# Attention and channel mix on one core: the five engines' order lists searched anew

## The chip, the core and the metric

The kernel runs on one core of a Trainium2 chip. The metric is the device time of one execution in microseconds, the median of several runs; lower is better. A core has five instruction streams: TensorE (PE; its weight loads are shown as PEld), VectorE (DVE), ScalarE (ACT), GpSimd (POOL) and SyncE (SP). Each works off its own list in order and meets the others through semaphores. In this kernel POOL issues the loads, SP the stores and the DMA transposes.

## The reference

Batch 8, 8 heads, 576 tokens, head size 64. A sliding-window attention with a linear position bias feeds a channel mix:

```python
scores = scale * np.matmul(q, k.transpose(0, 1, 3, 2))          # per head, 576 x 576
mask = (rel >= 0) & (rel < 128)                                  # rel = query - key
attn = softmax(np.where(mask, scores + bias, -1e9))              # bias = -slope * |rel|
x = np.matmul(attn, v)                                           # heads side by side: 576 x 512
xk = mu_k * x + (1 - mu_k) * x_prev                              # x_prev: the token before
xr = mu_r * x + (1 - mu_r) * x_prev
k = np.maximum(xk @ w_k, 0)                                      # 512 -> 1024
out = sigmoid(xr @ w_r) * ((k * k) @ w_v)                        # 1024 -> 512
```

## The kernel before, in words

Attention runs over 32 pairs of heads: pair `it` is heads 2g and 2g+1 of batch b = it // 4. The channel mix runs over units of two batches (P = 0 to 3, 1152 tokens each), cut into column chunks (c0) and row tiles (c) of 128 tokens. The program first registers 1139 small operations with their engine, dependencies and the buffer ring that they take a slot of. A planner then issues them. For each engine a text list, `ORDER`, gives the order in which its operations must be issued; each operation may start only after the one before it in the list. So the lists are the program's order on each engine, and the waits between engines follow from dependencies and rings. The planner's costs only settle how the five lists interleave when the program is written.

The names in the lists, with the kernel line that shows them in the profile:

- POOL: `lql.b.w.i` loads q (i = 0) or k (i = 1) of half of a batch's heads by token (L130), `lqp`, part of batch 0 (L119), `lqn.b.i.j` a block of 128 tokens for batches 4 to 7 (L88), `lts.b.i` the last 64 tokens (L124), `lvs.b.j` the blocks of V (L110, the last one L114), `lwk`, `lwr`, `lwv` the weights. `clear0`, `ms` and `clear` set ones and zeros in buffers (L441 to L447, L873, L875).
- SP: `lq`, `lmu` first loads; `tr.b.i` the DMA transpose of q or k of batch b in 4 to 7 (L93), `trt.b.i` of its tail (L98); `st.P.c` the store of a tile (L371).
- PE: `tq`, `tk`, `tail` transposes (L158, L171), `score.it.e` the scores of half of the keys (L219; pairs 0 to 3 add the bias by a matmul, L198), `av` (L250), `ot` the transpose of the result (L270), `m1.P.c0.fo` the product with w_k (L313; `m1a` its first three matmuls), `m3.P.c` with w_r (L336), `m2a` and `m2` the two halves of the product with w_v (L351; the last two tiles in column halves, L358), `fill` filler matmuls on zeros (L182), `tmu` a small transpose.
- ACT: `mask0` (L415), `pq` copies of q and k out of PSUM (L138), `exp` (L227), `xt` (L275), `rl` the relu (L319), `rs` the gate (L342), a few squares `kk`.
- DVE: `c`, `ct` casts by token (L149), `pk` (L135), `mcopy`, `dcopy`, `sid`, `id8`, `cmu` (constants), `mask` (L232), `norm` (L261, L262), `xk` (L295 and L302), `xr` (L302), `kk` the square (L328), `oo`, `oob` the product with the gate (L366).

Rings and buffers that couple the lists: `sa` (2 slots) holds scores and AV products in PSUM, `mm` (3 slots) the products of m1, m2 and m3, `ot` (4 slots) the tiles that wait for their store, three buffers hold V by batch, two hold q and k by batch (`ql`), and one (`qt`) holds the transposed q and k of a batch in 4 to 7. So `lqn` of batch 4 waits until `ct` of batch 2 has read the buffer, `lqn` of batch 6 until `tr` of batch 4 has, and `tr` of batch b until all scores of batch b-1 that used `qt` are done.

Of the kernel before, what the change touches and what calls it, by code (L numbers as in the profile page):

```python
# [16 lines left out]
def kernel(  # L17
# [704 lines left out]
    for i, m in enumerate(FILL):  # L722
# [4 lines left out]
            tq.0 tk.0 fill.0 tq.2 tail.0 score.0.0 score.2.0 tq.3 tmu score.2.1 score.0.1 av.2.0  # L727
            av.0.0 tq.1 score.3.0 score.3.1 av.0.1 ot.0.0 score.1.0 av.3.0 ot.0.1 av.2.1 tail.1
            ot.2.0 score.1.1 av.1.0 ot.3.0 av.3.1 ot.2.1 fill.1 av.1.1 ot.1.0 fill.2 ot.1.1
            m1a.0.0.0 ot.3.1 m1.0.0.0 m1.0.0.3 m1.0.0.2 tq.4 m1a.0.0.1 m1.0.0.4 m1.0.0.1 m1.0.0.5  # L730
            score.4.0 score.4.1 m1.0.256.0 tq.5 m1.0.256.3 m1.0.256.6 score.5.0 score.5.1 m1.0.0.6
            m1.0.256.5 m1.0.256.4 tq.6 m1.0.256.7 av.4 score.6.0 m1.0.256.1 ot.4 av.5 score.6.1
            tq.7 m3.0.2 m3.0.1 m1.0.256.2 ot.5 score.7.1 score.7.0 tail.2 m1.0.0.7 m3.0.0 tq.8
            av.6 m3.0.3 av.7 tq.9 m2a.0.0 m2a.0.1 ot.6 score.8.1 score.8.0 m2a.0.3 ot.7 m2.0.0
            m2.0.1 score.9.1 score.9.0 m2.0.3 m1.0.512.0 tq.10 m1.0.512.4 m1.0.512.1 m1.0.512.2
            av.8 m1.0.512.5 m2a.0.2 score.10.1 score.10.0 m1.0.512.7 ot.8 m2.0.2 av.9 tq.11
            m1.0.512.6 m1.0.512.3 m3.0.4 score.11.1 score.11.0 m3.0.8 ot.9 m3.0.6 m3.0.5 tq.12
            m1.0.768.0 av.10 m1.0.768.1 tq.13 m1.0.768.2 m1.0.768.7 score.12.0 score.13.0 m2a.0.4
            tail.3 ot.10 av.11 m2.0.4 tq.14 score.12.1 m2a.0.5 score.14.1 tq.15 m2.0.5 score.13.1
            score.14.0 m1.0.768.3 ot.11 m1.0.768.5 av.12 m1.0.768.4 m1.0.768.6 score.15.0  # L740
            score.15.1 m3.0.7 ot.12 av.13 m1.1.0.0 av.14 score.17.0 m1.1.0.7 score.18.0 score.16.1
            m2a.0.6 score.18.1 m2.0.6 score.17.1 m2a.0.7 av.15 score.16.0 m1.1.0.5 ot.13
            score.19.1 score.19.0 m2a.0.8 m2.0.7 ot.14 m2.0.8 m3.1.1 ot.15 m1.1.0.1 m1.1.0.6
            m3.1.0 m3.1.2 m1.1.0.4 m3.1.3 av.17 m1.1.512.0 av.16 m1.1.0.2 m1.1.512.7 m1.1.0.3
            m1.1.512.4 m1.1.512.3 ot.16 av.18 av.19 m2a.1.2 m2a.1.3 ot.17 m2a.1.0 m2.1.2 m2.1.0
            m2.1.3 ot.18 m2a.1.1 score.21.1 score.20.0 ot.19 m2.1.1 score.22.1 m1.1.512.5
            m1.1.512.2 score.20.1 m3.1.4 m1.1.896.0 score.23.1 score.22.0 m3.1.6 m3.1.8 m1.1.512.6
            m1.1.512.1 score.21.0 score.23.0 m3.1.5 m1.1.896.2 m3.1.7 av.20 m2a.1.6 m1.1.896.6
            m2.1.6 ot.20 av.21 m1.1.896.4 m1.1.896.7 m2a.1.5 av.22 m2a.1.4 m2.1.5 ot.21 m2.1.4
            m1.1.896.3 m1.2.0.0 m1.1.896.1 m1.2.0.4 m1.2.0.1 m1.2.0.3 m1.1.896.5 m1.2.0.7 ot.22  # L750
            av.23 m3.2.0 m1.2.0.5 m1.2.0.2 m3.2.1 ot.23 m2a.1.8 m1.2.0.6 score.27.1 score.24.1
            m2.1.8 m3.2.2 score.25.0 score.26.0 m2a.1.7 m2a.2.0 score.26.1 score.25.1 m2.1.7
            m2a.2.1 score.24.0 score.27.0 m2.2.0 m2.2.1 m1.2.512.0 m3.2.3 m1.2.512.7 m1.2.512.6
            m1.2.512.5 m2a.2.3 av.24 m2a.2.2 m2.2.3 m3.2.6 m2.2.2 av.25 ot.24 m1.2.896.0 m3.2.4
            m1.2.512.2 m1.2.512.3 m1.2.512.4 av.26 m1.2.896.6 m1.2.896.7 m1.2.512.1 ot.25
            m1.2.896.1 m3.2.8 m1.2.896.3 m3.2.5 av.27 m1.2.896.5 ot.26 m3.2.7 m1.2.896.4 ot.27
            m2a.2.5 score.29.0 score.28.0 m2.2.5 m2a.2.4 score.31.1 score.28.1 m2.2.4 m2a.2.6
            score.30.0 score.29.1 m2.2.6 m1.2.896.2 m1.3.0.0 score.30.1 score.31.0 m1.3.0.1
            m1.3.0.5 av.28 m1.3.0.6 m3.3.2 m1.3.0.2 m1.3.0.4 ot.28 av.29 m3.3.3 m1.3.0.7 m1.3.0.3
            ot.29 m2a.2.8 av.30 m2.2.8 m2a.2.7 ot.30 av.31 m2.2.7 m3.3.0 m3.3.1 m2a.3.2 ot.31  # L760
            m2a.3.3 m2.3.2 m2.3.3 m1.3.512.0 m2a.3.1 m2a.3.0 m2.3.1 m2.3.0 m1.3.512.2 m1.3.512.1
            m1.3.512.7 m3.3.4 m3.3.8 m1.3.512.5 m1.3.512.4 m1.3.512.6 m1.3.512.3 m1.3.896.0 m3.3.7
            m1.3.896.7 m3.3.5 m1.3.896.2 m2a.3.5 m2a.3.4 m2.3.5 m2.3.4 m1.3.896.1 m3.3.6
            m1.3.896.3 m1.3.896.6 m1.3.896.5 m2a.3.6 m1.3.896.4 m2.3.6 m2a.3.8 m2.3.8 m2a.3.7
            m2.3.7
        """,
        "ACT": """
            mask0.6 pq.0 mask0.4 mask0.2 mask0.0 pq.2 exp.0.0 exp.2.0 pq.3 exp.2.1 exp.0.1 pq.1
            exp.3.0 xt.0.0 exp.3.1 xt.0.1 exp.1.0 xt.2.0 xt.3.0 exp.1.1 xt.2.1 xt.1.0 xt.1.1
            xt.3.1 rl.0.0.0 rl.0.0.3 rl.0.0.2 pq.4 rl.0.0.4 rl.0.0.1 rl.0.0.5 exp.4.0 exp.4.1 pq.5  # L770
            rl.0.256.0 rl.0.256.3 rl.0.256.6 exp.5.0 rl.0.0.6 exp.5.1 pq.6 rl.0.256.5 rl.0.256.4
            exp.6.0 xt.4 rl.0.256.1 rl.0.256.7 exp.6.1 pq.7 rs.0.2 rs.0.1 rl.0.256.2 xt.5 exp.7.1
            exp.7.0 pq.8 rl.0.0.7 rs.0.3 rs.0.0 pq.9 xt.6 exp.8.1 xt.7 exp.8.0 exp.9.1 exp.9.0
            rl.0.512.0 rl.0.512.4 rl.0.512.1 kk.0.512.1 pq.10 rl.0.512.2 rl.0.512.5 exp.10.1 xt.8
            kk.0.512.5 exp.10.0 rl.0.512.7 pq.11 rl.0.512.3 rl.0.512.6 rs.0.4 exp.11.1 rs.0.8 xt.9
            rs.0.6 exp.11.0 pq.12 rs.0.5 rl.0.768.0 rl.0.768.1 pq.13 rl.0.768.2 kk.0.768.1
            exp.12.0 rl.0.768.7 xt.10 exp.13.0 pq.14 exp.12.1 exp.14.1 pq.15 exp.13.1 xt.11
            rl.0.768.3 exp.14.0 rl.0.768.5 rl.0.768.4 exp.15.0 kk.0.768.5 exp.15.1 rl.0.768.6
            rs.0.7 rl.1.0.0 exp.17.0 exp.18.0 exp.16.1 exp.18.1 exp.17.1 rl.1.0.7 xt.12 exp.16.0
            rl.1.0.5 kk.1.0.5 xt.13 xt.14 exp.19.1 xt.15 rs.1.1 rl.1.0.1 kk.1.0.1 rl.1.0.6 rs.1.0  # L780
            rs.1.2 exp.19.0 rs.1.3 rl.1.0.4 rl.1.512.0 rl.1.0.2 rl.1.512.7 rl.1.0.3 rl.1.512.4
            rl.1.512.3 xt.16 xt.17 xt.18 exp.21.1 exp.20.0 exp.22.1 rl.1.512.5 rl.1.512.2 exp.20.1
            kk.1.512.5 rl.1.896.0 rs.1.4 exp.23.1 rs.1.6 exp.22.0 rs.1.8 rl.1.512.6 rl.1.512.1
            exp.21.0 kk.1.512.1 rs.1.5 xt.19 rl.1.896.2 exp.23.0 rs.1.7 rl.1.896.6 rl.1.896.4
            rl.1.896.7 xt.20 rl.1.896.3 rl.2.0.0 rl.1.896.1 rl.2.0.4 kk.1.896.1 rl.2.0.1 xt.21
            kk.2.0.1 rl.1.896.5 rl.2.0.3 rl.2.0.7 kk.1.896.5 rs.2.0 rl.2.0.5 xt.22 rl.2.0.2
# [6 lines left out]
            exp.31.0 rl.3.0.2 rs.3.2 xt.28 rl.3.0.4 rs.3.3 rl.3.0.3 rl.3.0.7 xt.29 xt.30 rs.3.0
            rs.3.1 xt.31 rl.3.512.0 rl.3.512.2 rl.3.512.1 rl.3.512.7 rs.3.4 rs.3.8 rl.3.512.5
            rl.3.512.4 rl.3.512.6 rl.3.512.3 rl.3.896.0 rs.3.7 rl.3.896.7 rs.3.5 rl.3.896.2
            rl.3.896.1 rs.3.6 rl.3.896.3 rl.3.896.6 rl.3.896.5 rl.3.896.4
        """,
        "DVE": """
            id8 c.0.0 c.0.1 sid dcopy pk.0 ct.2 mcopy.2 pk.2 tcopy.0 ct.3 pk.3 ct.1 cmu mcopy.1
            norm.0.0 pk.1 mcopy.0 norm.2.0 norm.0.1 xk.0.0 norm.3.0 norm.2.1 tcopy.1 norm.1.0 ct.4  # L800
            xk.2.0 norm.3.1 norm.1.1 xk.1.0 xk.3.0 xk.2.1 xk.1.1 kk.0.0.0 xk.0.1 kk.0.0.2 kk.0.0.3
            xk.3.1 ct.5 kk.0.0.4 kk.0.0.1 xr.3 kk.0.0.5 xr.2 xr.1 ct.6 mask.4.0 kk.0.256.0
# [193 lines left out]
```

## Time and profile before

| what | value |
|---|---|
| median of 3 runs | 238.65 us (238.22 to 239.57) |
| the profiled execution, first to last instruction | 237.9 us |
| PE busy | 223.9 us, 94% |
| DVE busy | 193.2 us, 81% |
| ACT busy | 165.7 us, 70% |
| POOL busy | 93.2 us, 39% |
| chain that ended last | PE 76%, DVE 13%, DMA 3%, ACT 3% |
| DMA | 31.56 MB in 114810 packets |

No separate time is given for the profiled execution; its span is 0.75 us below the median of the runs. Busy is the share of the span in which an engine had an instruction in work. A row of the timeline gives the start in us, the length in us, the engine, the line, the operation, out<-in, the shape and the count; in brackets the idle time of the engine before it and what ended it. The granted clock of TensorE is 1.000 throughout.

### The profile page before, as it was taken

To read this page: it belongs to the slowest core of one execution; us is meant where nothing else is said; L and a number is where in the kernel's file an instruction comes from. 1 tells how busy PE (TensorE), PEld (TensorE's weight loads), DVE (VectorE), ACT (ScalarE), POOL (GpSimd) and SP (SyncE) were. 2 spreads that over 40 slices of the span, in tenths; PEclk is the share of its full clock that TensorE was granted. 3 is DMA by queue.
4 is the path that set the end of the run, shared out by engine and by line. 5 is a ranking of instruction groups with operands and counts; after the bars stand their busy time and mean duration, and the time that the engine had idled before them with its cause. 6 is when DMAs were issued, how large, how long until landed. Compare 5 with 4: busy or idle time off the path is not lost.

```text
span 237.9 us, 5426 instructions
## 1 busy us (share of the span) xinstructions
PE 223.9 (94%) x2130; PEld 132.9 (56%) x2163; DVE 193.2 (81%) x406; ACT 165.7 (70%) x281; POOL 93.2 (39%) x131
## 2 busy tenths in 40 slices
...
GB/s 131 166 137 184 178 160 200 188 159 210 202 139 149 134 164 135 125 123 212 193 171 184 123 123 181 193 77 148 99 90 3 118 19 0 91 0 132 0 91 178
DMA packets 114810, 31.56 MB, mean 133 GB/s; under 512 B 99160, under 2 KB 110432, under 8 KB 114784
## 3 DMA queue, kind: packets, MB, share of 16 engines
...
## 4 chain that ended last, share of the span: by engine, by line
PE 76%; DVE 13%; DMA 3%; ACT 3%; issue 2%; POOL 1%; POOLq 0%; DVEq 0%
PE pv L351 23%; PE ps L313 22%; PE pr L336 13%; PE sa L250 6%; PE sa L219 5%; PE tp L270 3%; DMA ql<-in_k_dram 3%; DVE at L232 2%; DVE xu L262 2%; DVE xk L302 2%; ACT at L227 2%; PE pv L358 1%; PE tp L158 1%; DVE ct L149 1%; DVE xr L302 1%
## 5 line engine op out<-in xcount | busy, mean ns | idle before, releaser
L313 PE MATMUL ps<-xk,wk_sb 128*128 128x256 bf16 (+2 forms) x410 | 71.9, 313 | 0.7 <-DVE xk L302 0.4
L319 ACT ACTIVATE rl<-ps 128x256 bf16<-128x256 f32 (+2 forms) x104 | 47.6, 476 | 31.1 <-PE ps L313 27.0
L227 ACT ACTIVATE at<-sa 128x1024 bf16<-128x1024 f32 x64 | 64.3, 1035 | 4.1 <-PE sa L219 3.9
L351 PE MATMUL pv<-wv_sb,kk 128*128 128x512 bf16 x257 | 63.9, 379 | 1.3 <-issue 0.6
L313 PEld LDWEIGHTS <-wk_sb 128*128 128x128 bf16 x416 | 38.7, 98 | 24.2 <-issue 2.0
L351 PEld LDWEIGHTS <-kk 128*128 128x128 bf16 x272 | 24.3, 98 | 24.3 <-issue 1.5
L232 DVE TENSOR_TENSOR at<-at,mask 128x1024 bf16<-128x1024 bf16 x56 | 37.5, 683 | 0.5 <-ACT at L227 0.2
L328 DVE TENSOR_TENSOR kk<-rl 128x256 bf16<-128x256 bf16 (+2 forms) x88 | 28.3, 335 | 10.7 <-ACT rl L319 10.1
L336 PE MATMUL pr<-wr_sb,xr 128*128 128x512 bf16 x135 | 35.6, 380 | 0.5
L366 DVE SCALAR_TENSOR_TENSOR ot<-rs,pv 128x512 f32<-128x512 bf16 (+1 forms) x38 | 24.5, 656 | 11.2 <-PE pv L351 4.9
L110 POOL DMA_DIRECT2D vs<-in_v_dram x32 | 28.6, 904 | 6.0 <-PE tp L270 2.4
L275 ACT COPY xt<-tp 128x576 bf16<-128x576 bf16 (+2 forms) x36 | 21.3, 590 | 13.4 <-PE tp L270 13.3
L302 DVE SCALAR_TENSOR_TENSOR xk<-dl,mu_sb,xt 128x576 bf16<-128x576 bf16 (+2 forms) x36 | 27.1, 752 | 1.3
L342 ACT ACTIVATE rs<-pr 128x512 bf16<-128x512 f32 x36 | 21.7, 611 | 8.8 <-PE pr L336 8.7
L302 DVE SCALAR_TENSOR_TENSOR xr<-dl,mu_sb,xt 128x576 bf16<-128x576 bf16 x32 | 25.5, 811 | 0.0
L250 PEld LDWEIGHTS <-at 128*128 128x128 bf16 x576 | 21.2, 98 | 6.4 <-issue 2.4
L262 DVE TENSOR_TENSOR xu<-sa,rc 128x640 bf16<-128x640 f32 x28 | 23.1, 824 | 1.0
L250 PE MATMUL sa<-vs,at 128*128 128x65 bf16 x448 | 18.9, 194 | 1.9 <-ACT rl L319 1.9
L336 PEld LDWEIGHTS <-xr 128*128 128x128 bf16 x144 | 13.4, 98 | 13.0 <-issue 0.6
L88 POOL DMA_DIRECT2D ql<-in_k_dram x16 | 14.2, 894 | 14.8 <-DMA qt<-ql 11.0
L138 ACT COPY qk<-tp 128x1024 bf16<-128x1024 bf16 (+1 forms) x16 | 14.7, 917 | 6.1 <-DVE qk L135 3.8
L295 DVE TENSOR_TENSOR dl<-xt 128x576 bf16<-128x576 bf16 (+2 forms) x36 | 15.1, 418 | 3.0 <-ACT xt L275 3.0
...
## 6 DMA issues: line engine op xcount, KB each, us to landing
out_dram<-ot SPq DMA_DIRECT2D x34, 256.0 KB, 3.8
...
ql<-in_q_dram POOLq DMA_DIRECT2D x7, 256.0 KB, 8.3
ql<-in_k_dram POOLq DMA_DIRECT2D x7, 256.0 KB, 7.6
wk_sb<-in_moe_w_k_dram POOLq DMA_DIRECT2D x2, 512.0 KB, 8.7
wv_sb<-in_moe_w_v_dram POOLq DMA_DIRECT2D x2, 512.0 KB, 10.2
```

The lines of the kernel that those rows point to most:

```text
L110: nc.gpsimd.dma_start(out=vs_buf[b % NLD][:, j, :, 0:D], in_=v[b, :, 128 * j:128 * j + 128, :].rearrange("h p d -> p h d"))
L227: nc.scalar.activation(out=at_half(it, e), in_=T.pop(("sa", it, e)), func=AF.Exp, scale=float(scale))
L232: nc.vector.tensor_tensor(out=at_half(it, e), in0=at_half(it, e), in1=mask[:, 2 * g:2 * g + 2, 256 * e:256 * e + 512], op=ALU.mult)
L250: nc.tensor.matmul(pa[:, hl, W * (t - t0):W * (t - t0) + W], lhsT=at[:, lo:lo + 128], rhs=vs[:, u, 2 * g + hl, :] if u < NF else tvb[:, 2 ...
L262: nc.vector.tensor_tensor(out=xu[:, t0:t1].rearrange("p t h d -> p h t d"), in0=a5[:, :, :, 0:D], in1=rc[:, :, 0:n, None].to_broadcast([12 ...
L302: nc.vector.scalar_tensor_tensor(out=to, in0=T["dl", it][:, c0:c1], scalar=mu_sb[:, NPO * which + g:NPO * which + g + 1], in1=xp, op0=ALU. ...
L313: nc.tensor.matmul(ps[:, 0:c1 - c0], lhsT=wk_sb[:, po, 128 * fo:128 * fo + 128], rhs=xk[:, po, c0:c1], start=(po == 0), stop=(po == NPO - 1))
L319: nc.scalar.activation(out=rl[:, 0:c1 - c0], in_=T.pop(("ps", P, c0, fo))[:, 0:c1 - c0], func=AF.Relu, scale=RELU_SCALE)
L328: nc.vector.tensor_tensor(out=T["kk", P, c0][:, fo, 0:c1 - c0], in0=rl[:, 0:c1 - c0], in1=rl[:, 0:c1 - c0], op=ALU.mult)
L336: nc.tensor.matmul(pr, lhsT=T["xr", P][:, po, 128 * c:128 * c + 128], rhs=wr_sb[:, po], start=(po == 0), stop=(po == NPO - 1))
L351: nc.tensor.matmul(pv, lhsT=kk[:, fo, o:o + 128], rhs=wv_sb[:, fo], start=(fo == 0), stop=(fo == NFO - 1))
L366: nc.vector.scalar_tensor_tensor(out=T["ot", P, c][:, w0:w1], in0=T["rs", P, c][:, w0:w1], scalar=1.0, in1=pv[:, 0:w1 - w0], op0=ALU.add, ...
```

## The change

All five texts of `ORDER` are replaced. The 1139 operations, their instructions, dependencies, rings and buffers stay. No list keeps its order over any length; what the text below speaks of, old (-) and new (+), cut:

```diff
 "PE":
-tq.0 tk.0 fill.0 tq.2 tail.0 score.0.0 score.2.0 tq.3 tmu score.2.1 ...
-ot.2.0 score.1.1 av.1.0 ot.3.0 av.3.1 ot.2.1 fill.1 av.1.1 ot.1.0 fill.2 ot.1.1 m1a.0.0.0 ot.3.1 m1.0.0.0 ...
+tq.0 fill.0 fill.1 tmu fill.2 tk.0 score.0.0 tq.2 tail.0 score.2.0 tq.3 score.0.1 ...
+ot.2.0 score.1.1 av.3.1 ot.3.0 av.1.0 ot.2.1 av.1.1 ot.1.0 ot.3.1 ot.1.1 m1a.0.0.0 tq.4 m1.0.0.0 ...
 "PE", around av.12:
-m2a.0.4 tail.3 ot.10 av.11 m2.0.4 tq.14 score.12.1 m2a.0.5 score.14.1 tq.15 m2.0.5 score.13.1 score.14.0 m1.0.768.3 ot.11 m1.0.768.5 av.12 ...
+score.13.0 score.13.1 m1.0.768.7 tq.14 m3.0.6 m1.0.768.2 tq.15 av.11 av.12 m1.0.768.4 m2a.0.5 score.14.0 score.14.1 m2.0.5 ...
 "ACT":
-mask0.6 pq.0 mask0.4 mask0.2 mask0.0 pq.2 exp.0.0 exp.2.0 pq.3 exp.2.1 exp.0.1 pq.1 exp.3.0 xt.0.0 exp.3.1 xt.0.1 exp.1.0 xt.2.0 xt.3.0 exp.1.1 ...
+mask0.2 mask0.4 mask0.0 mask0.6 pq.0 pq.2 exp.0.0 exp.2.0 pq.3 exp.0.1 exp.3.0 pq.1 exp.3.1 xt.0.0 exp.2.1 xt.0.1 exp.1.0 xt.2.0 exp.1.1 xt.3.0 ...
 "DVE":
-id8 c.0.0 c.0.1 sid dcopy pk.0 ct.2 mcopy.2 pk.2 tcopy.0 ct.3 pk.3 ct.1 cmu mcopy.1 norm.0.0 pk.1 mcopy.0 ...
+sid c.0.0 id8 mcopy.2 c.0.1 mcopy.0 dcopy pk.0 cmu ct.2 ct.3 pk.2 mcopy.1 tcopy.0 pk.3 ct.1 norm.0.0 pk.1 ...
-norm.15 kk.1.0.0 mask.16.1 xk.12 mask.16.0 oo.0.7 kk.1.0.7 oo.0.8 xk.14 mask.17.1 xk.13 xk.15 ...
+norm.15 kk.1.0.3 kk.1.0.7 mask.17.0 xr.12 oo.0.8 mask.16.0 kk.1.0.4 oo.0.7 xk.14 xk.15 xr.14 mask.16.1 ...
 "POOL":
-lql.0.1.0 lql.0.1.1 lts.0.0 clear0 lts.0.1 lqp.1.1 lvs.0.1 lqp.1.0 lvs.0.0 lvs.0.2 lvs.0.4 lvs.0.3 lts.1.1 ms ...
+clear0 lql.0.1.0 ms lql.0.1.1 lts.0.0 lqp.1.1 lts.0.1 lvs.0.0 lvs.0.1 lqp.1.0 ...
-lvs.2.0 lqn.4.0.1 lqn.4.0.3 lqn.4.0.2 lqn.4.0.0 lql.3.0.1 lql.3.0.0 lqn.4.1.3 lqn.4.1.1 lqn.4.1.2 lqn.4.1.0 lql.3.1.0 lts.3.1 lts.3.0 lql.3.1.1 lvs.3.3 lts.4.0 lvs.3.2 lts.4.1 lvs.3.4 lvs.3.1 lvs.3.0 lvs.4.2 ...
+lvs.2.4 lvs.3.4 lts.3.1 lql.3.1.0 lql.3.0.0 lql.3.0.1 lvs.3.2 lvs.3.0 lts.3.0 lqn.4.1.1 lts.4.1 lqn.4.1.2 lqn.4.0.0 lql.3.1.1 lqn.4.1.3 lts.4.0 lvs.3.1 lqn.4.0.2 lqn.4.1.0 lvs.3.3 lqn.4.0.3 lqn.4.0.1 lqn.6.0.2 lqn.5.0.2 lqn.5.1.3 lvs.4.1 lqn.5.1.0 lvs.4.2 lvs.4.0 lqn.5.1.2 lqn.5.0.1 lts.5.0 lqn.5.1.1 lts.5.1 lvs.4.3 lvs.4.4 ...
 "SP":
-lq.0.0 lmu.0 lq.0.1 lmu.1 st.0.1 st.0.3 st.0.2 tr.4.0 st.0.0 tr.4.1 trt.4.0 trt.4.1 st.0.4 trt.5.1 tr.5.1 tr.5.0 ...
+lq.0.0 lmu.0 lq.0.1 lmu.1 trt.4.0 st.0.0 st.0.1 trt.4.1 tr.4.1 tr.4.0 st.0.5 st.0.3 st.0.2 tr.5.1 st.0.6 ...
```

More of the change, by code (lines that the diff above doesn't have):

```diff
@@ L726 @@
         "PE": """
[L727 to L765, printed above, removed]
+            tq.0 fill.0 fill.1 tmu fill.2 tk.0 score.0.0 tq.2 tail.0 score.2.0 tq.3
+            score.0.1 av.2.0 av.0.0 score.3.0 tq.1 score.3.1 score.2.1 av.0.1 ot.0.0
+            av.3.0 score.1.0 ot.0.1 tail.1 av.2.1 ot.2.0 score.1.1 av.3.1 ot.3.0
@@ new lines @@
+            av.1.0 ot.2.1 av.1.1 ot.1.0 ot.3.1 ot.1.1 m1a.0.0.0 tq.4 m1.0.0.0 m1.0.0.3
+            score.4.1 m1a.0.0.1 m1.0.0.1 tq.5 m1.0.0.7 tail.2 m1.0.0.6 score.5.0
+            m1.0.256.0 score.5.1 tq.6 m1.0.0.4 score.4.0 m1.0.256.6 m1.0.0.2
+            m1.0.256.5 score.6.1 m1.0.256.3 tq.7 m1.0.256.4 score.6.0 av.4 m1.0.0.5
+            m3.0.2 av.5 score.7.1 ot.4 m3.0.3 score.7.0 ot.5 m1.0.256.1 av.6 m3.0.1
+            tq.8 av.7 m1.0.256.2 m1.0.256.7 tq.9 score.8.0 score.8.1 m3.0.0 ot.6
@@ new lines @@
+            m2a.0.0 ot.7 m2.0.0 m2a.0.1 m2a.0.3 score.9.0 score.9.1 tq.10 m2.0.1 av.8
+            m1.0.512.0 m2.0.3 score.10.0 score.10.1 ot.8 m1.0.512.5 m1.0.512.1
+            m1.0.512.3 av.9 m1.0.512.4 m2a.0.2 tq.11 m2.0.2 m1.0.512.7 ot.9 score.11.0
+            score.11.1 m1.0.768.0 tail.3 m3.0.7 tq.12 m1.0.512.6 m3.0.8 av.10 tq.13
+            m1.0.768.3 score.12.0 score.12.1 m3.0.4 m1.0.512.2 m3.0.5 m1.0.768.5 ot.10
+            score.13.0 score.13.1 m1.0.768.7 tq.14 m3.0.6 m1.0.768.2 tq.15 av.11 av.12
@@ new lines @@
+            m1.0.768.4 m2a.0.5 score.14.0 score.14.1 m2.0.5 m1.0.768.6 ot.11
+            score.15.0 score.15.1 m1.0.768.1 m2a.0.4 av.14 av.13 m2.0.4 ot.12 m1.1.0.0
+            m2a.0.6 score.18.0 score.16.1 m1.1.0.6 m2.0.6 score.17.0 score.17.1
+            m1.1.0.3 m1.1.0.7 ot.13 score.16.0 score.18.1 m1.1.0.4 m2a.0.8 av.15
+            m1.1.0.5 m2.0.8 ot.14 m2a.0.7 score.19.0 score.19.1 ot.15 m2.0.7 m3.1.0
+            m1.1.0.2 m1.1.0.1 m3.1.2 m1.1.512.0 m3.1.1 av.17 av.16 m1.1.512.1 m3.1.3
@@ new lines @@
+            m1.1.512.7 m1.1.512.3 ot.16 m1.1.512.2 m1.1.512.4 m2a.1.0 m2a.1.1 m2.1.0
+            av.19 av.18 m2.1.1 m2a.1.3 m2a.1.2 ot.17 score.22.0 score.20.0 m2.1.2
+            m2.1.3 score.21.1 score.21.0 m3.1.6 m3.1.4 m1.1.896.0 score.22.1
+            score.20.1 m1.1.512.6 m1.1.512.5 m3.1.5 m1.1.896.4 score.23.0 score.23.1
+            m2a.1.5 ot.18 m2.1.5 m2a.1.6 ot.19 m2.1.6 m1.1.896.3 m3.1.7 m1.1.896.2
+            m2a.1.4 m3.1.8 m2.1.4 av.21 m1.1.896.7 m1.1.896.1 m1.1.896.5 m1.1.896.6
@@ L769 @@
[L769 to L786, printed above, removed]
@@ L793 @@
[L793 to L796, printed above, removed]
+            mask0.2 mask0.4 mask0.0 mask0.6 pq.0 pq.2 exp.0.0 exp.2.0 pq.3 exp.0.1
+            exp.3.0 pq.1 exp.3.1 xt.0.0 exp.2.1 xt.0.1 exp.1.0 xt.2.0 exp.1.1 xt.3.0
```

163 lines of the change are left out of this document (107 added, 56 removed).

## The prediction

> **What bounds the kernel now.** I read the page's totals first, then busy time by stretches, then each wait of TensorE, then the chain of waits, then DMA landings.
>
> ```profile
> PE 223.9 (94%) x2130; PEld 132.9 (56%) x2163; DVE 193.2 (81%) x406; ACT 165.7 (70%) x281; POOL 93.2 (39%) x131
> core 0: us, PE busy (x) PEld busy (x) DVE busy (x) ACT busy (x) POOL busy (x), PEclk, DMA share, GB/s
> 0.00:24.90 24.90, 20.43 (x210) 10.68 (x214) 18.14 (x57) 15.60 (x27) 23.33 (x46) 1.00 1.60 155
> 24.90:38.00 13.10, 11.00 (x135) 8.46 (x133) 12.89 (x34) 12.03 (x22) 7.37 (x10) 1.00 1.89 173
> 38.00:79.00 41.00, 40.31 (x481) 26.56 (x487) 38.91 (x80) 37.72 (x60) 25.47 (x32) 1.00 1.87 174
> 79.00:84.00 5.00, 3.15 (x40) 1.93 (x39) 2.90 (x6) 3.18 (x6) 2.80 (x4) 1.00 2.09 141
> 84.00:234.40 150.40, 148.97 (x1279) 85.31 (x1296) 119.95 (x232) 97.13 (x168) 34.23 (x41) 1.00 1.16 114
> 234.40:237.90 3.50, 0.01 (x1) 0.00 (x0) 0.42 (x1) 0.00 (x0) 0.00 (x0) 1.00 0.33 114
> ```
>
> An order change adds and removes no instruction, so TensorE's 223.9 us stay and only its idle time can move. The stretches tell where that lies. Up to 24.90, where the first channel-mix matmul starts, it is 4.47 us and the engines feed each other in a chain. From 24.90 to 38 it is 2.10, with DVE (12.89 of 13.10) and ACT (12.03) nearly full: they bound that stretch. From 38 to 79 it is 0.69, from 79 to 84 it is 1.85, from 84 to the last matmul 1.43 in 150 us, and the tail (last product, last store) is 3.50. So from 84 on TensorE alone bounds the kernel and a new order has almost nothing to win there, only to lose. What can be won is one hole at 80 and the start.
>
> ```profile
> 81.83 0.62 PE L250 MATMUL sa<-vs,at 128*128 128x65 bf16 x15 [1.85 <-ACT rl L319]
> 65.20 1.77 POOL L110 DMA_DIRECT2D vs<-in_v_dram  x2
> L110 POOL DMA_DIRECT2D vs<-in_v_dram x1: 898/898/898, 66.1 to 66.1; - x1
> DMA to landing us min/median/max: 15.6/15.6/15.6
> 61.87 5.51 SPq L93 DMA_TRANSPOSE qt<-ql  x1
> 68.17 6.95 SPq L93 DMA_TRANSPOSE qt<-ql  x1
> ```
>
> The hole is av.12, the first AV product of batch 3. The profile names ACT's relu, but av.12 reads no relu. It reads vs of batch 3, whose last load (lvs.3.0, the second of the pair at 65.20) was issued at 66.1 and landed 15.6 us later, at 81.7; TensorE goes on at 81.83. That load was in flight while SP pushed the two transposes of batch 4 (tr.4.0 at 61.87, tr.4.1 at 68.17). I read the hole as a late load, slowed by the transposes.
>
> **The change, part by part.** *Loads and transposes (POOL, SP).* The new POOL list brings all of batch 3's loads in among batch 4's and puts lqn.4.0.1, which tr.4.0 needs, last of these 21. lqn.4.1.1 waits for ct.10 and ct.11, and what POOL issues later queues behind it.
>
> ```profile
> 49.19 0.89 DVE L149 COPY ct<-ql 128x1024 bf16<-128x1024 bf16 x2
> 94.09 1.80 POOL L110 DMA_DIRECT2D vs<-in_v_dram  x2
> DMA to landing us min/median/max: 7.6/7.8/7.9
> 104.80 0.62 PE L250 MATMUL sa<-vs,at 128*128 128x65 bf16 x15
> 113.78 3.45 PE pv L351 x16
> ```
>
> DVE does ct.11 and ct.10 at 49.19 to 50.08. The new DVE list has 15 instructions more ahead of them (four masks, three products, two xk and so on, less xr.4): at 38.91/80 = 0.486 us each, 7.3 us, so they end at about 57. From there lvs.3.3, now the last V load of batch 3, is ten issues on: 57 + 10 x 0.9 = 66, and it lands 7.8 us later (the pair at 94.09, loads beside no transpose in its first part), at 73.8; at 15.6 it would be 81.6. TensorE wants it at av.12. Without the hole that is 79.98, and in the new list 16 matmuls of m2 (3.45 us, the row at 113.78), one transpose block, two score blocks and an m1 that were ahead of av.12 are behind it, against one m3 (a quarter of that row, 0.86) the other way: about 76. 73.8 is in time by 2 us, since no transpose can start before about 72 now. Taken: -1.85. Ends: 0 and -1.85.
>
> *What that order costs.* The next POOL entry, lqn.6.0.2, reuses the buffer that tr.4.0 reads, so POOL stands until tr.4.0 has landed; queued behind it are the V loads of batch 4, which av.17 needs.
>
> ```profile
> 108.66 0.88 POOL L88 DMA_DIRECT2D ql<-in_k_dram  x1 [11.03 <-DMA qt<-ql]
> 95.70 11.63 SPq L93 DMA_TRANSPOSE qt<-ql  x2
> DMA to landing us min/median/max: 9.3/10.9/12.4
> 158.47 4.49 SPq L93 DMA_TRANSPOSE qt<-ql  x2
> DMA to landing us min/median/max: 4.8/4.8/4.8
> ```
>
> Such a wait lasts 11.03 us at 108.66 today and costs TensorE nothing. The new one: lqn.4.0.1 goes out at about 67.5 and lands at 75.3. If the transposes then go as the pair at 158.47 (2.2 us to issue, 4.8 to land), tr.4.0 lands at about 81; if as the pair at 95.70 (5.8 and up to 12.4), tr.4.1 issues 72 to 78 and tr.4.0 lands at 90. lvs.4.4 is 13 issues behind (11.7 us) and 7.8 in flight: 19.5 after. av.17 stands at 104.80; the new list has two m1 of 512 and one of 384 more and one m3 less ahead of it (+1.5), and the hole is gone (-1.85): 104.4. So tr.4.0 must land by 84.9. At 81 nothing is lost, at 90 TensorE waits 5.1. I take 81 and 0, the row at 158.47 being the nearer: with POOL standing there is no load beside tr.4.0. Stores behind the transposes on SP come out 5 us later or more, but their buffers are asked for again only some 10 us on.
>
> *The start.* POOL now clears buffers first: clear0 ahead of the first load, the ones and zeros of `ms` ahead of the second.
>
> ```profile
> 2.23 6.88 DMA ql<-in_k_dram
> 3.72 0.75 POOL L441 MEMSET tv<- 64x520 bf16 x1
> 4.63 0.39 POOL L447 MEMSET tt<- 128x256 bf16 x1
> 11.99 0.60 POOL L873 MEMSET at<- 128x64 bf16 x4
> 12.53 0.14 POOL L875 MEMSET xt<- 128x8 bf16 x2
> DMA to landing us min/median/max: 4.9/4.9/4.9
> 11.91 1.95 ACT L227 ACTIVATE at<-sa 128x1024 bf16<-128x1024 f32 x2
> 18.11 0.37 ACT L275 COPY xt<-tp 128x256 bf16<-128x256 bf16 x1 [0.42 <-PE tp L270]
> 19.73 0.43 ACT L275 COPY xt<-tp 128x320 bf16<-128x320 bf16 x1 [0.32 <-PE tp L270]
> 21.98 1.03 ACT L227 ACTIVATE at<-sa 128x1024 bf16<-128x1024 f32 x1
> ```
>
> clear0 runs 3.72 to 5.02 (1.30), ms 11.99 to 12.67 (0.68): the second load issues 1.98 later, at 4.21. It lands between 9.1 (the 4.9 of the tail load that follows it today; no delay) and 11.1 (its own 6.88; +1.98); I take the middle, +1.0. That load heads the chain through ct.2 to pq.2 and the first exponential at 11.91. pk.2 now stands behind ct.3, some +0.3. From there ACT's list is eight exponentials, three copies of q and k and a few xt; today it takes 11.91 to 23.01 (end of the last, 21.98 + 1.03), with ACT idle 0.42 and 0.32 in front of xt copies that come too early. The new list runs exp.3.1 ahead of xt.0.0 and moves xt.3.0 (0.37) behind the last exponential: -1.1. Start: +0.2, ends -0.8 and +2.3.
>
> The ten filler matmuls all move ahead of tk.0.
>
> ```profile
> 1.19 3.60 PE L182 MATMUL wm<-zero 128*128 128x512 bf16 x8 [1.19 <-DVE zero L435]
> 7.06 2.34 PE L182 MATMUL wm<-zero 128*128 128x512 bf16 x5
> 10.04 0.62 PE L158 MATMUL tp<-ident,ct 128*128 128x128 bf16 x8 [0.65 <-DVE ct L149]
> ```
>
> At 0.43 us each (3.60 for eight, less the last one's overlap; 2.34 for five) ten take 4.3 us from 5.0, so tk.0 ends near 9.8, pk.0 at 10.5, and ct.2 waits behind pk.0 and cmu until 10.9 instead of 10.2: +0.7. At the pace of 10.04 (eight 128-wide transposes in 0.62, half the time) they take 2.2 and nothing is lost. The trace does not tell which, as TensorE idled between 5.2 and 6.66; both lie within the start's ends, and I add 0.1. [...]
>
> *24.9 to 38.* The same four pairs' exponentials, copies, masks and norms are due there, and DVE and ACT are full in both lists, so I leave the 2.10 as it is (ends 0 and -2.1). One transpose block (ot.3.1) moves ahead of the first m1, where TensorE is idle anyway: -0.15.
>
> *DVE.* The list does more ahead of mask.16.1 than now: four kk, two masks, two products, four xk and two xr, 18 instructions.
>
> ```profile
> 94.92 0.68 DVE L232 TENSOR_TENSOR at<-at,mask 128x1024 bf16<-128x1024 bf16 x1
> 82.58 0.22 DVE L261 RECIPROCAL rc<-sa 128x10 f32<-128x10 f32 x1 [2.07 <-PE sa L250]
> 106.00 0.62 PE L250 MATMUL sa<-vs,at 128*128 128x65 bf16 x15
> ```
>
> At 119.95/232 = 0.517 us they take 9.3, so mask.16.1 moves from 94.92 to 104.2; DVE's own 2.07 us of waiting at the hole go: 102.1, done at 102.8. av.16 now starts at 106.00; with two m1 more and one m3 less (+0.86) and the hole gone it is 105.0. 2.2 us of room; I charge 0.3 for it and for other close meetings.
>
> *Tail.* Last kk, two m2 pairs of cover, two tiles in halves, last product, last store: the same work in the same places, 0.
>
> Sum: -1.85 + 0.2 + 0.1 - 0.15 + 0.3 = -1.4. The profiled span of 237.9 becomes 236.5. The median of the runs is 238.65, 0.75 above the span; 237.25, so 237.2.
>
> **Rivals.** (a) *POOL behind tr.4.0* (ends slower). Place: lqn.6.0.2 to av.17, point: tr.4.0 landing after 84.9. Each us beyond is a us of TensorE; at 90 the sum is +5.1 - 1.4, 242.3; half-way, at 87.5, +2.6 - 1.4 gives 239.9. For it: transposes took 5.5 to 6.95 us of SP in four of the issues shown. Against: all of those ran beside loads. (b) *The start pays the gain back*: load at +1.98, fillers at half rate and nothing won on ACT: +2.3 + 0.7 - 1.7 = +1.3, 239.95; with half of ACT's gain 239.4. For it: TensorE's chain is serial there. Against: ACT's idle rows. (c) *The hole is not a load's* or moves on: V of batch 3 lands late again (15.6) or DVE is late at av.16 by some 2 us: the -1.85 is lost, 239.1. Against: 81.7 and 81.83 agree to 0.13. (d) *The early stretch also packs better*: half of its 2.10 goes, and the load lands at 9.1: -1.4 - 1.05 - 1.0, 235.2.
>
> **How the numbers follow.** About 0.5% (1.2 us) is what a measurement of this kernel can tell from no change, so faster is below 237.46 and slower above 239.84. Forecast 0.43 (own range 236.3 to 238.2), (a) 0.17, (b) 0.15, (c) 0.12, (d) 0.13. Faster: two thirds of the forecast 0.30, all of (d), and a little of (b): 0.46. Slower: most of (a), some of (b): 0.20. Same: 0.34. The range leaves out the far half of (a) and the edge of (d): 234.9 to 240.0.
>
> **What would show it.** Right: no wait of a us or more of TensorE from 38 on, av.12 near 76, lvs.3.3 landing by 74; POOL idle for over 8 us before lqn.6.0.2 with nothing of it on TensorE; first m1 at 24.7 to 25.7. Wrong: an AV product of batch 4 released by a V load, a first exponential after 13.5, TensorE waiting for masks around 100, or over 2 us of new idle time after 84, where I have charged almost none.

## The result, and the profile after

The changed kernel runs in 237.39 us (median of 17 runs), the kernel before in 239.24 beside it: 0.9923 of the time, 95% interval 0.9899 to 0.9947, so 1.8 us faster (1.3 to 2.4). That is more than the 0.5% that can be told from no change. All ratios leave out the executions that are over 1.5% above the fastest of their kernel. The profiled run took 236.73 us, 235.0 of it span, so 1.73 lies around the span.

Busy time by stretches, the changed kernel (stretch, its length, then busy us and instructions of PE, PEld, DVE, ACT and POOL, granted clock, DMA share, GB/s):

```profile
0.00:24.90 24.90, 19.91 (x213) 10.83 (x216) 18.64 (x58) 16.01 (x28) 23.94 (x48) 1.00 1.49 157
24.90:38.00 13.10, 11.89 (x147) 8.47 (x147) 12.90 (x32) 12.00 (x22) 7.65 (x11) 1.00 1.73 184
38.00:79.00 41.00, 40.15 (x479) 27.36 (x486) 39.82 (x83) 38.13 (x64) 19.27 (x24) 1.00 1.83 158
79.00:84.00 5.00, 4.95 (x70) 3.35 (x70) 4.89 (x12) 4.63 (x7) 1.24 (x2) 1.00 0.60 196
84.00:231.50 147.50, 146.34 (x1231) 84.03 (x1249) 116.18 (x224) 93.94 (x163) 40.72 (x49) 1.00 1.08 119
231.50:235.00 3.50, 0.03 (x1) 0.00 (x0) 0.42 (x1) 0.00 (x0) 0.00 (x0) 0.96 0.22 77
```

TensorE's idle time: 1.21 us from 25 to 38 (2.10 before), 0.85 to 79 (0.69), 0.05 to 84 (1.85), 1.16 to the end (1.43), tail 3.50 as before. Up to 24.9 it is 4.99 against 4.47, but TensorE is also busy 0.52 less there: the first channel-mix matmul starts at 24.93, before at 24.89. So the span's 2.9 us are the hole (1.80), the early stretch (0.89) and 0.2 of the rest.

The longest waits of TensorE, the changed kernel (us in total, times, longest):

```profile
PE sa L219 <- ACT qk L138: 1.6, 3, 0.7
PE tp L270 <- ACT xt L275: 1.6, 3, 0.6
PE wm L182 <- DVE zero L435: 1.2, 1, 1.2
PE tp L158 <- DVE ct L149: 0.7, 1, 0.7
PE sa L250 <- DMA tv<-in_v_dram: 0.5, 1, 0.5
```

The wait of 1.2 us at L182 is the first filler's, at the very start, and the kernel before has it too. No other wait reaches 1 us, and the 1.9 us at L250 are gone. The last V load of batch 3, the two large transposes of batch 4, and TensorE around av.12 (the first x15 is the head of av.11, the second that of av.12):

```profile
L110 POOL DMA_DIRECT2D vs<-in_v_dram x1: 911/911/911, 66.6 to 66.6; - x1
DMA to landing us min/median/max: 6.3/6.3/6.3
73.23 5.10 SPq L93 DMA_TRANSPOSE qt<-ql  x2
```

```profile
74.78 0.62 PE L250 MATMUL sa<-vs,at 128*128 128x65 bf16 x15
75.24 0.19 PE L250 MATMUL sa<-tv,at 128*128 128x65 bf16 x1
75.27 0.19 PE L250 MATMUL sa<-vs,at 128*128 128x65 bf16 x1
75.30 0.20 PE L250 MATMUL sa<-tv,at 128*128 128x65 bf16 x1
75.33 0.62 PE L250 MATMUL sa<-vs,at 128*128 128x65 bf16 x15
```

The load lands at 72.9, av.12 starts at 75.3 with no pause. The large transposes start only when the load has landed; the small ones of the tails start at 68.61 and 71.80, within its flight, and it takes 6.3 us all the same.

### The profile page after: what moved, and what is told of

Read it like the earlier page. It is cut to its first block, busy times and chain, and to the rows that moved or that the text cites. A ratio compares the mean times of both kernels' runs of the same rounds, so it can differ in the third digit from the quotient of the medians.

```text
span 235.0 us, 5432 instructions
## 1 busy us (share of the span) xinstructions
PE 223.3 (95%) x2132; PEld 134.0 (57%) x2163; DVE 192.8 (82%) x406; ACT 164.7 (70%) x281; POOL 92.8 (40%) x131
## 4 chain that ended last, share of the span: by engine, by line
PE 75%; DMA 10%; POOL 8%; DVE 4%; issue 1%; POOLq 0%
PE ps L313 24%; PE pv L351 23%; PE pr L336 12%; PE sa L250 5%; DMA tv<-in_v_dram 5%; PE sa L219 5%; DMA wv_sb<-in_moe_w_v_dram 5%; PE tp L270 3%; POOL ql L130 2%; POOL ts L124 2%; POOL vs L110 2%; PE pv L358 1%; DVE xk L302 1%; DVE xu L262 1%; PE tp L158 1%
## 5 line engine op out<-in xcount | busy, mean ns | idle before, releaser
L313 PE MATMUL ps<-xk,wk_sb 128*128 128x256 bf16 (+2 forms) x410 | 73.8, 313 | 0.5 <-DVE xk L302 0.2
L351 PE MATMUL pv<-wv_sb,kk 128*128 128x512 bf16 x261 | 65.2, 379 | 0.7 <-issue 0.2
L319 ACT ACTIVATE rl<-ps 128x256 bf16<-128x256 f32 (+2 forms) x104 | 48.4, 479 | 20.8 <-PE ps L313 16.7
L313 PEld LDWEIGHTS <-wk_sb 128*128 128x128 bf16 x416 | 37.9, 98 | 21.5 <-issue 1.2
L351 PEld LDWEIGHTS <-kk 128*128 128x128 bf16 x272 | 25.4, 98 | 25.6 <-issue 0.6
L328 DVE TENSOR_TENSOR kk<-rl 128x256 bf16<-128x256 bf16 (+2 forms) x88 | 27.6, 335 | 14.9 <-ACT rl L319 14.7
L232 DVE TENSOR_TENSOR at<-at,mask 128x1024 bf16<-128x1024 bf16 x56 | 37.0, 684 | 0.2 <-ACT at L227 0.2
L88 POOL DMA_DIRECT2D ql<-in_q_dram x16 | 14.5, 926 | 27.0 <-DMA qt<-ql 26.3
L250 PEld LDWEIGHTS <-at 128*128 128x128 bf16 x576 | 21.2, 98 | 4.7 <-issue 0.6
L250 PE MATMUL sa<-vs,at 128*128 128x65 bf16 x448 | 18.7, 194 | 0.1
```

Source lines behind the costliest of these rows:

```text
L232: nc.vector.tensor_tensor(out=at_half(it, e), in0=at_half(it, e), in1=mask[:, 2 * g:2 * g + 2, 256 * e:256 * e + 512], op=ALU.mult)
L250: nc.tensor.matmul(pa[:, hl, W * (t - t0):W * (t - t0) + W], lhsT=at[:, lo:lo + 128], rhs=vs[:, u, 2 * g + hl, :] if u < NF else tvb[:, 2 ...
L313: nc.tensor.matmul(ps[:, 0:c1 - c0], lhsT=wk_sb[:, po, 128 * fo:128 * fo + 128], rhs=xk[:, po, c0:c1], start=(po == 0), stop=(po == NPO - 1))
L319: nc.scalar.activation(out=rl[:, 0:c1 - c0], in_=T.pop(("ps", P, c0, fo))[:, 0:c1 - c0], func=AF.Relu, scale=RELU_SCALE)
L328: nc.vector.tensor_tensor(out=T["kk", P, c0][:, fo, 0:c1 - c0], in0=rl[:, 0:c1 - c0], in1=rl[:, 0:c1 - c0], op=ALU.mult)
L351: nc.tensor.matmul(pv, lhsT=kk[:, fo, o:o + 128], rhs=wv_sb[:, fo], start=(fo == 0), stop=(fo == NFO - 1))
```

## The experiments

Lists are cut by entry numbers (`before[:16]` is the first 16 entries of that list in the kernel before, `PE[36:86]` the entries 37 to 86); ratios are to the kernel before.

**e1: the load order alone.**

```
 # before, with
-POOL = before
+POOL = changed
+SP   = changed places of loads and transposes, stores in the old order
```

> The kernel before with only the new order of loads and transposes (the POOL list and the places of SP's transposes); PE, ACT and DVE as before. Theory (the hole near 80 is V of batch 3 landing late, and the new load order alone cures it): the last V load of batch 3 is issued by 64 and lands by 74, av.12 starts near 80 without a wait, the 1.85 us go, ratio to before 0.992 (0.989 to 0.995). The 2.1 us of TensorE's idle time from 25 to 38 stay, since they belong to the lists of ACT and DVE. Rival (the gain of the change is spread over the compute lists, the loads carry none of it): ratio 1.000, and TensorE still waits over 1.5 us near 80.

Ratio 1.0034 (0.9992 to 1.0076): the rival's time, but not for its reason. TensorE by stretches and its longest wait:

```profile
7.00:10.10 3.10, 0.32 (x2) 0.00 (x0) 0.72 (x3) 0.68 (x3) 3.00 (x5) 0.95 1.89 164
10.10:16.00 5.90, 5.34 (x32) 2.49 (x32) 1.71 (x5) 2.39 (x3) 4.95 (x8) 0.50 3.08 135
79.00:84.00 5.00, 5.00 (x67) 3.08 (x66) 4.99 (x8) 5.00 (x8) 4.43 (x6) 1.00 0.90 145
```

```profile
PE tp L158 <- DVE ct L149: 3.2, 2, 2.9
```

The hole is gone, but with the old PE list nothing fills the time until ct.2: TensorE idles 2.87 us, and then works at a granted clock of 0.50 until about 16.6 (0.50 to 16, a mean of 0.84 from 16 to 18). The first channel-mix matmul is at 28.12, 3.2 us late. From it to av.12 (83.44) the kernel takes 55.32 us, before 56.94: 1.6 won, lost at the start. Three of the twelve executions kept a mean granted clock of 1.000; their spans are 236.6, 236.6 and 236.9 us, against 239.5 at 0.984 in the profiled one. So most of the loss is the halved clock, and it does not come in every execution.

**e5: the load order alone, without the start.**

```
-POOL = before
+POOL = before[:16] + the rest as changed
+SP   = as in e1
```

> As e1_loads_only, but POOL's first 16 entries stay as before (the clears behind the first loads); from the 17th entry on POOL, and on SP, the order is the changed kernel's; PE, ACT and DVE as before. Theory (the new load order cures the hole, and e1 lost its gain in the start alone, where TensorE idled 2.87 us before 10.18 and was then granted half its clock until about 16): the first channel-mix matmul is back at 24.3 to 25.4, no wait at av.12, no other of a us, ratio 0.992 (0.989 to 0.996), and the granted clock is 1.0 from 10 to 16. Rival (the new load order costs something of its own elsewhere): ratio 0.998 to 1.005 with a wait of a us or more that names its place.

```profile
24.90:38.00 13.10, 11.19 (x142) 8.61 (x141) 12.93 (x33) 11.77 (x22) 7.64 (x10) 1.00 1.71 185
79.00:84.00 5.00, 4.95 (x70) 3.33 (x69) 4.27 (x9) 4.88 (x8) 4.51 (x6) 1.00 1.26 178
```

0.9929 (0.9904 to 0.9955). The hole is gone by loads and transposes alone, with the compute lists untouched, the first channel-mix matmul is at 24.06 (24.3 to 25.4 expected), and the ratio cannot be told from the change's, though 1.9 us of idle time stay from 25 to 38.

**e4: only the transposes later.**

```
 SP, before:
-st.0.2 tr.4.0 st.0.0 tr.4.1 trt.4.0 trt.4.1 st.0.4
+st.0.2 st.0.0 trt.4.0 trt.4.1 st.0.4 tr.4.0 tr.4.1
```

> The kernel before with one edit: on SP the two large transposes of batch 4 move behind the store st.0.4, to about 79. Theory (the transposes slow the V loads of batch 3): without them in flight lvs.3.0, issued near 66, takes 8 to 11 us and not 15.6, lands by 77, and av.12 does not wait; the scores of batch 4 then wait for the transposes instead, some 5 to 10 us, so the whole is slower (244 to 252). Rival (the load is late because of the loads queued ahead of it, not the transposes): lvs.3.0 lands at 80 or later as before.

The last two V loads of batch 3, and TensorE's longest wait:

```profile
L110 POOL DMA_DIRECT2D vs<-in_v_dram x2: 881/886/890, 65.8 to 66.7; - x2
DMA to landing us min/median/max: 8.1/8.1/8.1
```

```profile
PE sa L219 <- DMA qt<-ql: 4.7, 1, 4.7
```

One run of 243.38, just below the 244 to 252 expected. The load that took 15.6 us takes 8.1 with the large transposes out of its way, lands at 74.8, and no wait at av.12 remains; the scores wait 4.7 us instead. So the transposes held the load back, as predicted; that it takes 6.3 in the changed kernel is beyond what this run explains.

**e3: V of batch 3 early, all else as before.**

```
 POOL, before:
-lvs.2.0 lqn.4.0.1
+lvs.2.0 lvs.3.3 lvs.3.2 lvs.3.4 lvs.3.1 lvs.3.0 lqn.4.0.1
...
-lql.3.1.1 lvs.3.3 lts.4.0 lvs.3.2 lts.4.1 lvs.3.4 lvs.3.1 lvs.3.0 lvs.4.2
+lql.3.1.1 lts.4.0 lts.4.1 lvs.4.2
```

> The kernel before with one edit: the five V loads of batch 3 move ahead of lqn.4.0.1 on POOL. Theory: they land by 60, the wait of 1.85 us at av.12 goes and nothing else comes in its place, ratio 0.992 (0.989 to 0.996). Rival 1 (the hole is not a load's): still 1.5 us or more near 80, ratio 1.000. Rival 2 (the loads pushed back, of batch 3's q and k and of batch 4, make a wait of their own, at ct.12 to ct.15 or at the first score of batch 4): the hole at av.12 goes and another of a us or more appears, ratio 0.996 to 1.01.

```profile
PE to L171 <- DMA ts<-in_q_dram: 1.9, 1, 1.9
```

```profile
73.00:75.00 2.00, 0.06 (x1) 0.03 (x1) 0.36 (x2) 0.40 (x2) 0.00 (x0) 1.00 1.63 216
75.00:77.00 2.00, 2.00 (x28) 1.88 (x29) 0.69 (x2) 1.02 (x2) 0.69 (x1) 0.56 1.72 160
77.00:79.00 2.00, 2.00 (x12) 1.00 (x10) 1.77 (x5) 0.54 (x1) 1.08 (x2) 0.59 1.42 174
```

1.0109 (1.0067 to 1.0150): rival 2 in kind, a shade beyond its range, and at a place that it did not name. The V loads land by 57 and av.12 doesn't wait; now the tail loads of batch 3, issued at 60.8 and 61.8, take 13 us beside the transposes, the last lands at 74.8, and TensorE waits 1.9 us for it. Behind that wait its granted clock is 0.56 and 0.59 for 4 us, which makes it dearer than the hole of before, after which the clock stayed at 1.00. Two of the twelve executions, with a mean clock of 0.998 and 1.000, have spans of 237.8 and 237.7 us; the other ten, at 0.983 to 0.993, have 240.2 or more. The hole went from one load beside the transposes to another.

**e2: the old load order in the changed kernel.**

```
 # changed, with
-POOL = changed
+POOL = before
+SP   = old places of loads and transposes, stores in the new order
```

> The changed kernel with the old order of loads and transposes; PE, ACT and DVE as changed. Theory: the new DVE list makes ct.11 at 57.4 and the old POOL list has lqn.4.0.1, which waits for it, ahead of 20 loads with all of V of batch 3 among the last; lvs.3.0 goes out near 75 and lands at 81 to 90, TensorE wants it at 75.3, so a wait of 6 to 15 us near 75 and a ratio to before of 1.02 to 1.06. Rival (load order does not matter much): ratio 0.992 as for the whole change.

```profile
PE to L171 <- DMA ts<-in_q_dram: 14.1, 2, 8.8
```

1.1085 (1.1013 to 1.1157), worse than expected and at another place: tail.2 and tail.3, which the new PE list has early, wait for tail loads that the old POOL list has late.

**e6: the old start; e8: the old stretch.**

```
 # e6: changed, with
+PE = before[:36], ACT = before[:24], DVE = before[:31], POOL = before[:16], the rest as changed
 # e8: changed, with
+PE[36:86], ACT[24:62] = before, 44 entries of DVE[31:78] in the order of before
```

> The changed kernel with the start of before on all engines (first 36 entries of PE, 24 of ACT, 31 of DVE, 16 of POOL: up to the first channel-mix matmul). Theory 1 (the start is neutral, the gain is the hole and the stretch from 25 to 38): first channel-mix matmul at 24.3 to 25.4, TensorE idle 1.0 to 1.5 us from 25 to 38, ratio to before 0.990 to 0.994, as the whole change. Theory 2 (the 0.9 us won from 25 to 38 come from exponentials that are done 1 us earlier in the new start): idle near 2.1 there, ratio 0.994 to 0.998. Rival (the new start costs, and without it the kernel gains more): ratio 0.985 to 0.989.

> The changed kernel with the order of before for what runs from about 25 to 42 on ACT (entries 25 to 62) and PE (37 to 86), and on DVE for the 44 of its entries 32 to 78 that both lists have there. Theory 1 (the new lists pack the DVE- and ACT-bound stretch from 25 to 38 better): TensorE idle near 2.1 us there, the hole near 80 stays gone, ratio to before 0.994 to 0.998. Theory 2 (the gain there comes with the new start): idle 1.0 to 1.5, ratio 0.990 to 0.994.

TensorE from 24.9 to 38, e6 and then e8:

```profile
24.90:38.00 13.10, 11.27 (x143) 7.97 (x141) 12.63 (x31) 11.44 (x21) 7.89 (x11) 1.00 1.77 183
```

```profile
24.90:38.00 13.10, 10.75 (x129) 8.20 (x127) 12.93 (x32) 11.50 (x21) 8.46 (x11) 1.00 1.72 184
38.00:79.00 41.00, 39.72 (x479) 26.90 (x487) 38.55 (x80) 37.57 (x61) 19.20 (x24) 1.00 1.74 152
```

e6: 0.9922 (0.9874 to 0.9969), first channel-mix matmul at 24.88: no gain or cost of the new start that these seven runs can tell. Its idle time of 1.83 in the stretch lies between the two theories' figures. e8: 0.9969 (0.9943 to 0.9996), idle 2.35, as theory 1 says; but 1.28 from 38 to 79, more than either kernel has, shows that the cut itself costs something.

**e12: the new stretch alone.**

```
 # before, with
+PE[36:86], ACT[24:62], DVE[31:78] = changed, entries left out behind them
```

> The kernel before with the changed kernel's order for the stretch from about 25 to 42 alone: PE's entries 37 to 86, ACT's 25 to 62, DVE's 32 to 78 (the three that only one of the lists has there go behind). Loads, transposes and start as before. Theory 1 (the new lists pack that stretch better by 0.9 us, independent of the loads): TensorE idle 1.0 to 1.5 us from 25 to 38 and not 2.1, the wait of 1.5 us or more near 80 stays or grows, since av.12 is asked for sooner and its load is no earlier: ratio to before 0.998 to 1.002, the gain of the stretch lost at the late load. Theory 2 (it is won for good): ratio 0.994 to 0.997. Rival (the packing only moves idle time to 38 to 79): idle there up by 0.5 us or more, ratio 0.999 to 1.004.

```profile
PE to L171 <- DMA ts<-in_q_dram: 5.9, 1, 5.9
```

1.0383 (1.0331 to 1.0435), none of the three: tail.2 stands early in the new stretch, its loads go out at 26.1 and 27.8 in the old order and land at 36.4 (changed: out at 13.7 and 14.5, landed by 19.6). This stretch can't be had without the new load order.

**e7: five fillers moved back.**

```
 PE, changed:
-tq.0 fill.0 fill.1 tmu fill.2 tk.0
+tq.0 fill.0 tmu tk.0
...
+ot.2.1 fill.1 av.1.1 ot.1.0 fill.2
```

> The changed kernel with two of the three blocks of filler matmuls (five of ten) moved back from the gap before tk.0 to their places of before, behind ot.2.1 and ot.1.0. Theory (the fillers now keep TensorE's granted clock up while ct.2 is awaited, but score.0.0, which the new list has in that gap, does so too): tk.0 1.0 to 1.4 us earlier, granted clock 1.0 throughout, first channel-mix matmul within 0.5 us of 24.9, ratio to before 0.990 to 0.995. Rival (without them the clock is halved as in e1 from about 10 on): first channel-mix matmul 2 to 3 us later, ratio 1.000 to 1.005.

0.9890 (0.9845 to 0.9935); first channel-mix matmul at 24.15, earlier than expected, ct.2 at 8.63, granted clock 1.0. So the new places of these five fillers are not what the clock of 1.0 hangs on here. With score.0.0 in the gap TensorE pauses 0.67 us ahead of tq.2, which reads ct.2; in e1 score.0.0 stands behind tq.2, the pause is 2.87 us, and a clock of 0.50 follows. No run moves score.0.0 alone.

**e9 and e11: POOL held up behind tr.4.0.**

```
+op(("dly",), "POOL", 5000, lambda: [nc.gpsimd.memset(dly, 0.0) for _ in range(3)])
-lqn.4.0.1 lqn.6.0.2
+lqn.4.0.1 dly lqn.6.0.2
 # e11: range(6), and
+lqn.4.0.1 lqn.6.0.2 dly
```

> The changed kernel with one addition: three memsets of a scratch tile of 128x1200 bf16 on POOL ahead of lqn.6.0.2, some 5 us (at the 0.75 us of a memset of 520 elements a row), as if tr.4.0 had landed that much later for POOL; nothing else waits for them. It prices the rival 'POOL behind tr.4.0'. By the prediction's point (84.9, where POOL goes on at 82.7 in the changed kernel) 2.2 us are free and TensorE waits the rest, 2.8 us of 5, at av.17 for a V load of batch 4: ratio to before 1.002 to 1.006. By the changed kernel's trace (last V load of batch 4 landed at 99.5, av.17 at 103.4) 3.9 us are free: a wait of 1.1 us, ratio 0.995 to 0.999. Rival (that wait is off the path altogether, or loads behind a longer gap come faster): no wait for a V load, ratio 0.990 to 0.994.

```profile
L949 POOL MEMSET dly<- x3: 1097/1097/1172, 68.2 to 70.6; 128x1200 bf16 x3
```

0.9918 (0.9886 to 0.9949), but it tells nothing: the memsets ran at 68 to 72, inside POOL's wait, and lqn.6.0.2 went out at 81.59 as it would have.

> The changed kernel with one addition: six memsets of a scratch tile of 128x1200 bf16 on POOL behind lqn.6.0.2 (in e9 three of them, ahead of it, took 1.10 us each and ran while POOL waited for tr.4.0 anyway, so they delayed nothing). Now they start when tr.4.0 has landed and delay the V loads of batch 4 by 6.6 us, as a landing of tr.4.0 at 89.3 would. By the prediction's point (84.9, so 2.2 us free) TensorE waits 4.4 us at av.17: ratio to before 1.009 to 1.013. By the changed kernel's trace (last V load of batch 4 landed at 99.5, av.17 at 103.4, 3.9 us free) it waits 2.7 us: ratio 1.001 to 1.006. Rival (the wait never reaches TensorE): no wait for a V load, ratio 0.990 to 0.994.

TensorE in e11 (the profiled execution took 241.78 us, the longest of the twelve; its granted clock was also 0.50 from 12 to 14 us and from 26 to 28, and all stands 1.3 us later than in the changed kernel), and two stretches:

```profile
104.87 0.50 PE L250 MATMUL sa<-vs,at 128*128 128x65 bf16 x11
106.73 0.28 PE L250 MATMUL sa<-vs,at 128*128 128x65 bf16 x4 [1.36 <-DMA vs<-in_v_dram]
107.45 0.19 PE L250 MATMUL sa<-tv,at 128*128 128x65 bf16 x1 [0.45 <-DMA tv<-in_v_dram]
```

```profile
105.00:107.50 2.50, 0.69 (x18) 0.51 (x16) 0.36 (x1) 1.24 (x3) 1.40 (x2) 1.00 2.65 120
107.50:111.00 3.50, 3.28 (x27) 2.06 (x28) 2.19 (x5) 0.95 (x2) 0.00 (x0) 0.51 1.55 162
```

0.9978 (0.9940 to 1.0015): by the ratios 0.55% or 1.3 us above the change (0.2 to 2.4). The mechanism is the prediction's, at av.17, for V of batch 4; the price is under both estimates, though the interval reaches the foot of the lower one. av.17 does not stop as a whole: 11 of its matmuls run on the tiles that are there and four more when the next has landed, and TensorE is idle 1.81 us, not 2.7.

**e10: another start**, tried to beat both kernels.

```
 POOL: -clear0 lql.0.1.0 ms lql.0.1.1 lts.0.0 lqp.1.1 lts.0.1
       +clear0 lqp.1.1 lqp.1.0 lql.0.1.0 lts.0.0 lts.0.1 lql.0.1.1 ms
 ACT:  -pq.0 pq.2 exp.0.0 exp.2.0 pq.3 exp.0.1
       +pq.0 mask0.4 mask0.0 pq.1 exp.0.0 exp.0.1 pq.2 exp.1.0
...
```

> The changed kernel with another order for its first part (the first 75 entries of PE, 50 of ACT, 64 of DVE, 30 of POOL): the two small loads of pair 1 ahead of the large ones of pairs 2 and 3, pair 1 taken second, exponentials of pair 0 in ACT's gap from 5.9 to 11.6, products and copies that nobody waits for later. Theory (the start is a chain from the second large load through ACT and DVE, and the large load lands no earlier whatever is ahead of it): the chain starts with pair 1 at 7 to 8, the first channel-mix matmul comes at 21.5 to 23.5 and not 24.9, ratio to before 0.980 to 0.988. Rival (bandwidth: the weights and batch 1's loads land when they land, so what the start wins TensorE waits from 25 to 45): ratio 0.989 to 0.995, idle time of TensorE from 25 to 45 up by 1 us or more.

```profile
22.50:38.00 15.50, 12.64 (x160) 9.73 (x162) 15.13 (x38) 13.34 (x25) 10.29 (x13) 1.00 1.70 183
```

0.9932 (0.9903 to 0.9962): the same as the change, and the rival's time. The first channel-mix matmul comes at 22.57, 2.4 us earlier, and TensorE then idles 2.86 us to 38; av.4 is 0.7 later than in the changed kernel. It is hardly bandwidth, as the rival had it: DVE is busy 15.13 of 15.50 us, and none of the waits of TensorE that the profile lists from 25 to 45 ends on a load. This start, which moves DVE's work back, gains nothing.

## Why the prediction was right, point by point

237.2 was predicted, 237.39 measured. The mechanism of the hole held; that the number is so near is in part luck, since two of its numbers were off and offset each other. In spans it went from 237.9 to 236.5, and the trace shows 235.0; and it put 0.75 us around the span, where the run shows 1.73. The old profile's own time was not at hand; its span was set against a median of other runs. In medians it is the same: the gain was 1.85 us and not 1.4, but from 239.24 (17 runs), where the forecast started from 238.65 (3 runs).

- *The hole* (-1.85): measured -1.80. The step held as argued: lvs.3.3 landed at 72.9 (73.8 predicted), av.12 started at 75.3 (76). e4 shows that the transposes held the load back, e5 that the load order alone removes the hole, e3 that a load in the wrong place takes it over.
- *The start* (+0.2): +0.04, by two sub-terms that both missed; that they offset is luck. The second load, issued at 3.56 and not 4.21, took 5.0 us and landed at 8.56, earlier than before (9.11): no delay, not +1.0. The exponentials end at 22.04, 1 us earlier as predicted (-1.1), but the first channel-mix matmul (24.93) did not follow: the transposes ahead of it wait for ACT's copy xt, and the matmuls behind it for xk on DVE.

```profile
24.77 0.33 PE L270 MATMUL tp<-ident,xu 128*128 128x128 bf16 x3 [0.51 <-ACT xt L275]
25.37 0.38 PE L313 MATMUL ps<-xk,wk_sb 128*128 128x256 bf16 x2 [0.16 <-DVE xk L302]
```

  The rival "the start pays the gain back" did not happen here; e1 shows that a start can cost as much, 3.2 us, but in another way: by idle time (2.87 us) and the halved clock (0.50 from 10.1 to 16), with the old PE list.
- *Fillers* (+0.1): the ten took 3.0 us, between the 4.3 and 2.2 reckoned: the first two lasted 634 ns each, the third, at 5.9, 467, and those from 6.2 on 379 to 390, though the profile gives a granted clock of 1.00 from 5 to 8.2. No run shows the 0.1 itself, which was the author's estimate. ct.2 started at 9.26, behind pk.0 and cmu, though its load had landed at 8.56; in e7, with five fillers fewer ahead, it started at 8.63 and the first channel-mix matmul 0.8 us earlier. So the fillers may have eaten what the earlier load won; e7's ratio shows no cost that can be told from none.
- *24.9 to 38* (0 taken, ends 0 and -2.1): the mis-sized term, -0.89 in the trace, with the -0.15 for ot.3.1 in it. e8 supports it, e12 shows that it hangs on the new load order; how much of it the medians hold stays open, since e5, without it, is as fast as the change within 0.4%. The executions with a mean granted clock of 0.998 or more point to about 1 us: their spans have medians of 236.2 us in e5 (8 of them), 235.3 in e6 (6), which has the new lists behind the start, and 237.4 in the kernel before beside them (11).
- *POOL behind tr.4.0* (0): it waited, hid, and had more room than reckoned.

```profile
POOL ql L88 <- DMA qt<-ql: 26.3, 2, 13.5
```

  POOL went on at 82.76 (81 taken); the V loads then needed 16.7 us and not 19.5, and the last landed at 99.5, 4.1 us ahead of av.17 (103.60). The point of this rival was nearer 86.9 than 84.9, and e11 puts its price below 1 us a us.
- *DVE* (+0.3): mask.16.1 ran at 102.61 to 103.29 (102.1 to 102.8 predicted), av.16 at 104.15 without a wait; not spent. *Tail* 0: 3.50 in both.
